# Moving a second gate rank, one attention stage and eight squares in a fused attention and two-layer MoE kernel

## The chip, the cores and the metric

The kernel runs on one core of one Trainium2 chip. The metric is the device time of one execution in microseconds (us). The kernel before takes 973.56 us, the median of three runs (973.33 to 974.96).

## The reference, cut to what matters

```python
# attention over chunks of 32 queries: 8 memory keys and a window of 16 + 32 + 8 keys
scores = scale * np.matmul(q_c, k_full.transpose(0, 1, 3, 2))
scores = scores - np.max(scores, axis=-1, keepdims=True)
a = np.exp(scores)
a = a / (np.sum(a, axis=-1, keepdims=True) + 1e-09)
out[:, :, c_start:c_end] = np.matmul(a, v_full)
# dense layer, 512 -> 2048 -> 512, on 3072 tokens
h = x @ w_in
r = np.maximum(h, 0.0)
x = (r * r) @ w_out
# top-1 mixture of 8 experts, 512 -> 1024 -> 512
e_idx = np.argmax(x @ w_gate, axis=1)
out[mask] = gate_w[mask, None] * eom[mask, e, None] * (np.maximum(x[mask] @ w1[e], 0.0) @ w2[e])
```

## The kernel before, in words

Tokens go in 12 blocks of 256 (two 128-token units each). A **duo** is the attention of one block, a **block** its dense layer. Every fp32 operand of a large product is split into a high and a low part, so a product is three matmuls. Two blocks form a group: group 1 is blocks 2 and 3, and so on. The list `seq` (L844 to L850) holds the work **items** (block, f), where f is one of 16 strips of the hidden layer. Items 0 to 31 are group 0, items 32 to 63 group 1, then 32 for each group to item 191; from item 192 on come pairs of 128-token tiles for one expert, then single tiles ("slots") to the end.

The main loop (L1114 to L1129) writes the order of every engine by hand; each engine runs its instructions in that order. For item n it issues: the first product `mm1_both` (12 matmuls, for two blocks at once, at every second item), work put `ahead`, the item's `relu`, then everything planned for n in `todo`, and last `mm2`, the second product (6 matmuls) of item n - 2. `relu` is on ScalarE (ACT) the relu `r` (L418) and the rounded square `gh` (L430), and on VectorE (DVE) the square `g` (L428) and the residual `gl` (L432). For items below 24 the square `g` is on ACT too (L426): at that time DVE also converts the weights (`split_w_or` L336 and L340, `split_w_lo` L354; `split_w_hi` L349 is on ACT).

`plan_duo(b, s, m, t, v)` places the attention of a block: scores (128 small matmuls of TensorE, PE, L158; maximum L187 and subtraction L192 on DVE, exponential L208 on ACT) at item s, the norm (L214 to L220, DVE) at m, the transposes (L231, PE) at t, the second attention product `av` (128 small matmuls, L256) at v. `plan_gate(b, y, l, c, r)` places the gate of a finished block: transposes, logits, choice, and `gate_rank` at r (L520): two small matmuls (L525, L526) give each token its place in its expert's list, seven small DVE operations follow, and two indirect DMAs from GpSimd (POOL, L537) scatter 128 rows of 8 bytes each into `listd` in HBM. `prepare` (L971) runs at item 23.

In group 1 (n = 32) the rank of the second gate stands at n + 27 and the second duo's `av` at n + 29; in groups 2 to 4 at n + 26 and n + 29.

Of the kernel before, what the change touches and what calls it, by code (L numbers as in the profile page):

```python
# [8 lines left out]
F32 = mybir.dt.float32  # L9
F32R = mybir.dt.float32r  # L10
BF16 = mybir.dt.bfloat16
# [6 lines left out]
P = 128  # L18
# [3 lines left out]
NE = 8  # L22
F2 = 1024
BLK = 256
NB = NT // BLK
TPB = BLK // P
# [16 lines left out]
C_ID, C_U, C_RANK, C_BASE, C_LT, C_ROW, C_SIG, C_TOK, C_ODD, C_NUM = 0, 128, 256, 264, 273, 435, 444, 467, 491, 506  # L43
# [11 lines left out]
def chunk_attention_relu2_moe_top1_kernel(ctx: ExitStack, tc, qk, vv, qt, kv, w_in, w_out, wg, wexp, consts, out):  # L55
    nc = tc.nc
# [9 lines left out]
    rp = ctx.enter_context(tc.tile_pool(name="rp", bufs=1))  # L66
# [6 lines left out]
    cst = cpool.tile([P, NCONST], F32, name="cst")  # L73
    ident = cst[:, C_ID : C_ID + P]
    wg_sb = cpool.tile([P, KC, 32], F32, name="wg_sb")
    before = cpool.tile([P, P], BF16, name="before")
# [289 lines left out]
    class Block:  # L366
# [52 lines left out]

        def relu_g(self, f):  # L420
            b = self.b
            early = at[b, f] < 24
            r = self.r
            g = gp.tile([P, BLK], F32, tag="g", name=f"g{b}_{f}")
            if early:
                nc.scalar.activation(g, r, ACTF.Square)  # L426
            else:
                nc.vector.tensor_tensor(g, r, r, op=ALU.mult)  # L428
            gh = gp.tile([P, BLK], F32R, tag="gh", name=f"gh{b}_{f}", bufs=3)
            nc.scalar.activation(gh, r, ACTF.Square)  # L430
            gl = gp.tile([P, BLK], F32R, tag="gl", name=f"gl{b}_{f}", bufs=3)
            nc.vector.tensor_tensor(gl, g, gh.bitcast(F32), op=ALU.subtract)  # L432
            self.g[f] = gh, gl
# [50 lines left out]
        def gate_choose(self):  # L484
            b = self.b
            ps = ps_h.tile([P, D], F32, tag="h", name=f"psg{b}")[:, : TPB * P]
            ps = ps.rearrange("p (t k c) -> p t k c", t=TPB, k=KC)
            for t in range(TPB):
                nc.tensor.transpose(
                    ps[:, t].rearrange("p k c -> p (k c)"), self.lt[:, t * P : t * P + P], ident  # L490
                )
            lg = rp.tile([P, TPB, 16], F32, tag="lg", name=f"lg{b}")
            nc.vector.tensor_reduce(
                out=lg, in_=ps.rearrange("p t k c -> p t c k")[:, :, 0:16, :], axis=AX.X, op=ALU.add
            )

            def small(name, *shape, dt=F32):
                return rp.tile([P, TPB, *shape], dt, tag=name, name=f"{name}{b}")

            mx, d, ev, first = small("gm"), small("gd", NE), small("gv", NE), small("gf")  # L500
            nc.vector.tensor_reduce(out=mx, in_=lg[:, :, 0:NE], axis=AX.X, op=ALU.max)
            nc.vector.tensor_tensor(d, lg[:, :, 0:NE], mx.unsqueeze(2).to_broadcast([P, TPB, NE]), op=ALU.subtract)
            rank = cst[:, C_RANK : C_RANK + NE].unsqueeze(1).to_broadcast([P, TPB, NE])
            nc.vector.scalar_tensor_tensor(ev, d, 0.0, rank, op0=ALU.is_ge, op1=ALU.mult)
            nc.vector.tensor_reduce(out=first, in_=ev, axis=AX.X, op=ALU.max)
            self.oh = small("oh", NE, dt=BF16)
            nc.vector.tensor_tensor(self.oh, ev, first.unsqueeze(2).to_broadcast([P, TPB, NE]), op=ALU.is_equal)

            ex, se, og, so = small("ge", NE), small("gs"), small("go", NE), small("gt")
            nc.scalar.activation(ex, d, ACTF.Exp)  # L510
            nc.vector.tensor_tensor(og, lg[:, :, NE : 2 * NE], self.oh, op=ALU.mult)
            nc.vector.tensor_reduce(out=so, in_=og, axis=AX.X, op=ALU.add)
            nc.scalar.activation(so, so, ACTF.Exp, scale=-1.0)
            nc.vector.tensor_reduce(out=se, in_=ex, axis=AX.X, op=ALU.add)
            nc.vector.tensor_scalar_add(so, so, 1.0)
            nc.vector.scalar_tensor_tensor(se, se, EPS, so, op0=ALU.add, op1=ALU.mult)
            nc.vector.reciprocal(ent[:, b * TPB : (b + 1) * TPB, 1].bitcast(F32), se)
# [333 lines left out]
    at = {bf: n for n, bf in enumerate(seq)}  # L851
# [3 lines left out]
    def plan(n, fn, *args):  # L855
        todo.setdefault(n, []).append((fn, args))

    def plan_duo(b, s, m, t, v, last=None):
        d = duos[b]
        plan(s, d.scores)  # L860
        plan(m, d.norm)
        plan(t, d.transpose_a)
        plan(v, d.av)
        if last is None:
            plan(v, d.transpose_x_copy)
        else:
            ahead[last] = d.transpose_x_copy
        if b + 1 < NB:
            plan(s + 1, duos[b + 1].load_q, 0)
            plan(s + 1, duos[b + 1].load_q, 1)  # L870
        if 2 < b < NB - 1:
            plan(v + 1, duos[b + 1].load_kv, 1)
        if b < NB - 2:
            plan(v + 2, duos[b + 2].load_kv, 0)

    def plan_gate(b, y, l, c, r):
        bl = blocks[b]
        plan(y, bl.gate_transpose)
        plan(l, bl.gate_logits)
        plan(c, bl.gate_choose)  # L880
        plan(r, bl.gate_rank)
# [17 lines left out]
    plan(bits[14] + 1, duos[3].load_kv, 0)  # L899
    plan(bits[15] + 1, duos[3].load_kv, 1)  # L900
    plan(23, lambda: prepare())
    n = at[2, 0]
    plan_duo(2, n - 8, n - 7, n - 4, n - 3)
    plan_duo(3, n + 1, n + 2, n + 5, n + 6)
    plan_gate(0, n + 7, n + 9, n + 15, n + 18)
    plan_duo(4, n + 11, n + 13, n + 15, n + 17)
    plan_gate(1, n + 19, n + 23, n + 25, n + 27)
    plan_duo(5, n + 21, n + 23, n + 25, n + 29, last=n + 30)
    for g in range(2, GROUPED - 1):
        n = at[2 * g, 0]  # L910
        plan_gate(2 * g - 2, n + 3, n + 5, n + 11, n + 15)
        plan_duo(2 * g + 2, n + 7, n + 9, n + 11, n + 13)
        plan_gate(2 * g - 1, n + 15, n + 17, n + 23, n + 26)
        plan_duo(2 * g + 3, n + 19, n + 21, n + 23, n + 29, last=n + 30)
    n = at[NB - 2, 0]
    plan_gate(NB - 4, n + 3, n + 4, n + 6, n + 9)
    plan_gate(NB - 3, n + 6, n + 8, n + 10, n + 12)
    n = at[NB, 0]
    plan_gate(NB - 2, n + 2, n + 3, n + 4, n + 6)
    plan_gate(NB - 1, n + 4, n + 5, n + 7, n + 8)  # L920
    pairs = [Pair(p) for p in range(NP)]
    slot = [Slot(s) for s in range(NS)]
    entries = pairs + slot
# [3 lines left out]
    last = at[NB, 0] - NF  # L927
# [12 lines left out]
    for p in range(NP):  # L940
        n = at[NB + p, 0]
# [24 lines left out]
    n = at[NB, 0]  # L966
# [4 lines left out]
    def prepare():  # L971

        nc.sync.dma_start(wg_sb, wg)
        nc.vector.tensor_copy(before, cst[:, C_U : C_U + P])
        nc.gpsimd.tensor_copy(base, cst[:, C_BASE : C_BASE + NE + 1])
        nc.gpsimd.tensor_copy(ent[:, :, 0], cst[:, C_TOK : C_TOK + NU])
        fill = tp.tile([P, ROWS // P, 2], I32, tag="t2", name="fill")
        nc.gpsimd.memset(fill[:, :, 0], NT)
        nc.gpsimd.memset(fill[:, :, 1], 0)
        nc.sync.dma_start(listd.rearrange("(p r) c -> p (r c)", p=P), fill.rearrange("p r c -> p (r c)"))  # L980
        zero = tp.tile([1, D], F32, tag="t2", name="zero")
        nc.gpsimd.memset(zero, 0.0)
        nc.sync.dma_start(ydram[NT : NT + 1, :], zero)

    with tc.manual_schedule():
# [4 lines left out]
        a, b = (0,), (1,)  # L990
# [276 lines left out]
```

## Time and profile before

| what | value |
| --- | --- |
| median of three runs | 973.56 us |
| profiled execution, its own time | 975.07 us |
| its span, first to last instruction | 973.3 us |
| PE busy | 951.2 us (98%) |
| DVE busy | 603.4 us (62%) |
| ACT busy | 450.2 us (46%) |
| POOL busy | 95.9 us (10%) |

The page's 40 slices show PE at 9 tenths or more nearly everywhere; the few 8s are at the start and at the fifth and tenth slices. Each engine's share is an average over stages: DVE stands at 9 tenths in the first four slices, at about 4 to 5 in the middle, and at 9 at the end. Times in the rows below count from the first instruction.

### The profile page before, as it was taken

The numbers are of one execution on the slowest core, as the hardware profiler recorded it, in microseconds if no ns is written. First come the engines' busy times: TensorE is split into PE (matmuls) and PEld (weight loads), VectorE is DVE, ScalarE is ACT, GpSimd is POOL, SyncE is SP. The second block draws the span as 40 slices with busy tenths as digits, with TensorE's granted clock in tenths as the row PEclk, the third lists the DMA queues.
The fourth block names the chain that finished last, engine by engine and source line by source line (L and its number), as shares of the span: only waits on it lengthen the run. The fifth ranks groups of instructions, "written<-read, shape, count | busy, mean of one in ns | idle before, by whom it ended". The sixth has DMA issues, their size and how long they took to land. (4 is left out here: it accounts for less than half of the span.)

```text
span 973.3 us, 19449 instructions
## 1 busy us (share of the span) xinstructions
PE 951.2 (98%) x7862; PEld 795.8 (82%) x7862; DVE 603.4 (62%) x1134; ACT 450.2 (46%) x808; POOL 95.9 (10%) x92
## 2 busy tenths in 40 slices
PE   8999899998999999999999999999999999999997
PEld 5787689877888888888888878888999999888885
DVE  6899753552455345544545344658776666799995
ACT  4687433322332333323333223544554454688885
POOL 0000000000000000000000001002222212122221
PEclk9999999998999999999999999999999999999999
DMA  9566422214120222103010104452775666553531
GB/s 357 180 232 238 151 102 110 88 23 87 66 88 23 52 80 69 63 5 127 23 45 1 45 1 173 173 217 66 297 303 227 231 221 243 187 198 130 216 123 42
DMA packets 30992, 129.06 MB, mean 133 GB/s; under 512 B 8559, under 2 KB 9071, under 8 KB 19122
## 3 DMA queue, kind: packets, MB, share of 16 engines
q1 hardware_dynamic: 25650, 113.84, 32.1%
q0 software_dynamic: 5248, 13.92, 4.2%
q8 instruction: 64, 1.05, 0.5%
q14 instruction: 30, 0.25, 0.1%
HBM read 142.19 MB, written 13.61 MB: 160 GB/s over the span
## 5 line engine op out<-in xcount | busy, mean ns | idle before, releaser
L386 PE MATMUL ph<-xhi,wi 128*128 128x512 f32 x688 | 213.6, 391 | 1.0 <-issue 0.7
L428 DVE TENSOR_TENSOR g<-r 128x256 f32<-128x256 f32 x168 | 70.8, 422 | 187.4 <-ACT r L418 187.4
L418 ACT ACTIVATE r<-ph 128x256 f32<-128x256 f32 x192 | 72.1, 375 | 238.9 <-PE ph L386 192.7
L443 PE MATMUL py<-wo,gh 128*128 128x512 f32 x384 | 157.1, 409 | 4.4 <-ACT gh L430 4.4
L386 PEld LDWEIGHTS ph<-xhi,wi 128*128 128x128 f32 x688 | 130.0, 189 | 29.7 <-DVE wi L354 1.1
L444 PE MATMUL py<-wo,gh 128*128 128x512 f32 x384 | 151.0, 393 | 0.0
L445 PE MATMUL py<-wo,gl 128*128 128x512 f32 x384 | 150.8, 393 | 0.0
L386 PE MATMUL ph<-xlo,wi 128*128 128x512 f32 x344 | 134.1, 390 | 0.0
L680 DVE TENSOR_TENSOR x<-raw,x 128x1024 fp32r<-128x1024 f32 x88 | 103.2, 1221 | 7.0 <-ACT x L679 5.4
L432 DVE TENSOR_TENSOR gl<-g,gh 128x256 fp32r<-128x256 f32 x192 | 81.6, 425 | 24.8 <-ACT gh L430 1.6
L680 DVE TENSOR_TENSOR p<-raw,p 128x1024 fp32r<-128x1024 f32 x64 | 78.2, 1221 | 22.3 <-ACT p L679 21.7
L443 PEld LDWEIGHTS py<-wo,gh 128*128 128x128 f32 x384 | 72.6, 189 | 21.1 <-ACT gh L430 5.2
L679 ACT CAST x<-raw 128x1024 fp32r<-128x1024 f32 x88 | 87.3, 1057 | 0.0
L445 PEld LDWEIGHTS py<-wo,gl 128*128 128x128 f32 x384 | 72.6, 189 | 16.2 <-DVE gl L432 0.4
L430 ACT ACTIVATE gh<-r 128x256 fp32r<-128x256 f32 x192 | 80.0, 416 | 11.2 <-PE py L444 3.0
L537 POOL DMA_INDIRECT listd<-ent,idx x24 | 25.2, 1051 | 590.5 <-DVE idx L535 341.1
L444 PEld LDWEIGHTS py<-wo,gh 128*128 128x128 f32 x384 | 72.9, 190 | 12.6
L386 PEld LDWEIGHTS ph<-xlo,wi 128*128 128x128 f32 x344 | 64.9, 189 | 13.7
L679 ACT CAST p<-raw 128x1024 fp32r<-128x1024 f32 x64 | 66.6, 1041 | 0.0
L831 PE MATMUL po<-x,ht 128*128 128x512 f32 x264 | 65.4, 397 | 0.6 <-DVE ht L821 0.6
L701 POOL DMA_INDIRECT out<-o,slots x27 | 36.0, 1335 | 209.4 <-ACT o L697 91.4
L831 PEld LDWEIGHTS po<-x,ht 128*128 128x128 f32 x264 | 48.1, 188 | 10.2 <-DVE ht L821 1.0
(229 smaller groups left out, 1453.8 us busy)
## 6 DMA issues: line engine op xcount, KB each, us to landing
raw<-in_wexp SPq DMA_DIRECT2D x82, 1024.0 KB
kv<-in_kv SPq DMA_DIRECT2D x19, 1024.0 KB
raw_o<-in_w_out SPq DMA_DIRECT2D x8, 1024.0 KB
raw_i<-in_w_in SPq DMA_DIRECT2D x7, 1024.0 KB
ydram<-y SPq DMA_DIRECT2D x24, 256.0 KB
q<-in_qt SPq DMA_DIRECT2D x20, 256.0 KB
qk<-in_qk SPq DMA_DIRECT2D x4, 768.0 KB
v<-in_vv SPq DMA_DIRECT2D x2, 1024.0 KB
```

The lines of the kernel that those rows point to most:

```text
L386: nc.tensor.matmul(ph.rearrange("p (s c) -> p s c", s=2), lhsT=w_in_part(w, f, k), rhs=x[:, s, k, :], start=(n == 0), stop=(n == 11),)
L418: nc.scalar.activation(self.r, self.ph, ACTF.Relu, scale=WSCALE)
L428: nc.vector.tensor_tensor(g, r, r, op=ALU.mult)
L430: nc.scalar.activation(gh, r, ACTF.Square)
L432: nc.vector.tensor_tensor(gl, g, gh.bitcast(F32), op=ALU.subtract)
L443: nc.tensor.matmul(self.y[t], lhsT=gh[:, s], rhs=w_out_part(wh, f), start=(f == 0), stop=False)
L444: nc.tensor.matmul(self.y[t], lhsT=gh[:, s], rhs=w_out_part(wl, f), start=False, stop=False)
L445: nc.tensor.matmul(self.y[t], lhsT=gl[:, s], rhs=w_out_part(wh, f), start=False, stop=(f == NF - 1))
L679: nc.scalar.copy(w[:, 0], t)
L680: nc.vector.tensor_tensor(w[:, 1], t, w[:, 0].bitcast(F32), op=ALU.subtract)
L701: nc.gpsimd.indirect_dma_start(out=out, out_offset=bass.IndirectOffsetOnAxis(ap=slots[:, c, 0:1].bitcast(U32), axis=0), in_=self.y[t], in_ ...
L831: nc.tensor.matmul(self.po, lhsT=self.ht[:, part, f, :], rhs=w[:, wp, j * D : j * D + D], start=(f == 0 and part == 0 and wp == 0), stop=( ...
```

## The change

The square `g` of items 24 to 31 goes from DVE to ACT. Duo 2's scores go from item 24 to 25 and its norm from 25 to 26; its transposes (28) and `av` (29) stay. In group 1 the second gate's logits go from n + 23 to n + 21 and its rank from n + 27 to n + 30; duo 5's scores go from n + 21 to n + 23, its norm from n + 23 to n + 24, its transposes from n + 25 to n + 27. In groups 2 to 4 the rank of the second gate goes from n + 26 to n + 30, one item behind `av`. After the groups, the rank of block 10 goes from item 198 to 199 and the choice of block 11 from 199 to 198, so the one-hot tile `oh` gets a second buffer. A cast in `prepare` goes from DVE to POOL.

```diff
         def relu_g(self, f):
             b = self.b
-            early = at[b, f] < 24
+            early = at[b, f] < 32
...
-            def small(name, *shape, dt=F32):
-                return rp.tile([P, TPB, *shape], dt, tag=name, name=f"{name}{b}")
+            def small(name, *shape, dt=F32, bufs=1):
+                return rp.tile([P, TPB, *shape], dt, tag=name, name=f"{name}{b}", bufs=bufs)
...
-            self.oh = small("oh", NE, dt=BF16)
+            self.oh = small("oh", NE, dt=BF16, bufs=2)
...
     n = at[2, 0]
-    plan_duo(2, n - 8, n - 7, n - 4, n - 3)
+    plan_duo(2, n - 7, n - 6, n - 4, n - 3)
     plan_duo(3, n + 1, n + 2, n + 5, n + 6)
     plan_gate(0, n + 7, n + 9, n + 15, n + 18)
     plan_duo(4, n + 11, n + 13, n + 15, n + 17)
-    plan_gate(1, n + 19, n + 23, n + 25, n + 27)
-    plan_duo(5, n + 21, n + 23, n + 25, n + 29, last=n + 30)
+    plan_gate(1, n + 19, n + 21, n + 25, n + 30)
+    plan_duo(5, n + 23, n + 24, n + 27, n + 29, last=n + 30)
     for g in range(2, GROUPED - 1):
         n = at[2 * g, 0]
         plan_gate(2 * g - 2, n + 3, n + 5, n + 11, n + 15)
         plan_duo(2 * g + 2, n + 7, n + 9, n + 11, n + 13)
-        plan_gate(2 * g - 1, n + 15, n + 17, n + 23, n + 26)
+        plan_gate(2 * g - 1, n + 15, n + 17, n + 23, n + 30)
         plan_duo(2 * g + 3, n + 19, n + 21, n + 23, n + 29, last=n + 30)
...
     n = at[NB, 0]
-    plan_gate(NB - 2, n + 2, n + 3, n + 4, n + 6)
-    plan_gate(NB - 1, n + 4, n + 5, n + 7, n + 8)
+    plan_gate(NB - 2, n + 2, n + 3, n + 4, n + 7)
+    plan_gate(NB - 1, n + 4, n + 5, n + 6, n + 8)
...
-        nc.vector.tensor_copy(before, cst[:, C_U : C_U + P])
+        nc.gpsimd.tensor_copy(before, cst[:, C_U : C_U + P])
```

## Rows read from the trace of the kernel before

**Rows 1.** The page, part 1: busy time, share and instructions of each engine.
```profile
PE 951.2 (98%) x7862; PEld 795.8 (82%) x7862; DVE 603.4 (62%) x1134; ACT 450.2 (46%) x808; POOL 95.9 (10%) x92
```

**Rows 2.** Waits of PE and POOL: line, what for, total us, times, longest us.
```profile
PE py L443 <- ACT gh L430: 4.4, 2, 3.6
PE ph1p L731 <- DVE gl1p L742: 0.8, 1, 0.8
...
POOL listd L537 <- DMA listd<-ent,idx: 40.5, 11, 7.5
```

**Rows 3.** Timeline around duo 2, 99 to 116 us: start, duration, engine, line, operation.
```profile
99.75 0.22 DVE L974 CAST before<-cst 128x128 bf16<-128x128 f32 x1
...
103.48 1.23 DVE L354 TENSOR_TENSOR wo<-ws_o,wo 128x1024 fp32r<-128x1024 f32 x1 [0.23 <-ACT wo L349]
...
104.63 1.22 DVE L187 TENSOR_REDUCE mx<-pss 128x16 f32<-128x1024 f32 x1
...
107.37 1.06 ACT L208 ACTIVATE e<-e 128x1024 f32<-128x1024 f32 x1 [3.92 <-DVE e L204]
108.33 0.36 ACT L418 ACTIVATE r<-ph 128x256 f32<-128x256 f32 x1
...
109.20 0.78 PE L443 MATMUL py<-wo,gh 128*128 128x512 f32 x1 [3.59 <-ACT gh L430]
...
109.63 1.21 DVE L214 TENSOR_REDUCE sm<-e 128x16 f32<-128x1024 f32 x1
...
111.37 1.22 DVE L220 TENSOR_TENSOR e<-e,rs 128x1024 f32<-128x1024 f32 x1
...
115.02 1.03 PE L231 MATMUL psa<-cst,e 128*128 128x128 f32 x8
```

**Rows 4.** The square on ACT, by line and shape: xcount, busy us, mean ns.
```profile
L426 ACT ACTIVATE g<-r 128x256 f32<-128x256 f32 x24 | 10.1, 419 | 0.8
```

**Rows 5.** Stretches of eighteen large matmuls: length, busy by engine (instructions), PE clock, DMA.
```profile
283.44:287.65 4.21, 4.21 (x26) 3.49 (x19) 1.22 (x1) 1.01 (x1) 0.00 (x0) 1.00 0.69 247
200.20:205.35 5.15, 4.44 (x27) 3.41 (x19) 2.37 (x2) 0.00 (x0) 0.96 (x1) 1.00 0.52 77
231.14:237.37 6.23, 6.23 (x20) 4.97 (x19) 0.00 (x0) 0.01 (x1) 0.00 (x0) 0.65 0.86 49
109.18:115.00 5.82, 5.80 (x18) 4.62 (x19) 4.73 (x9) 1.34 (x4) 0.00 (x0) 0.71 0.02 9
```

**Rows 6.** Five `av`, L256 alone: stretch, length, PE and PEld busy (instructions), clock.
```profile
281.44:283.44 2.00, 1.98 (x128) 1.96 (x128) 1.00 0.00 0
225.24:231.14 5.90, 3.27 (x128) 2.86 (x128) 0.79 0.03 3
331.98:334.67 2.69, 2.27 (x128) 2.15 (x128) 1.00 0.01 0
433.50:436.24 2.74, 2.30 (x128) 2.18 (x128) 1.00 0.07 6
535.13:537.41 2.28, 2.26 (x128) 2.15 (x128) 1.00 0.03 4
```

**Rows 7.** Timeline of group 1: scatters, the stopped `av`, item 63's relu.
```profile
203.16 0.96 POOL L537 DMA_INDIRECT listd<-ent,idx  x1 [7.52 <-DMA listd<-ent,idx]
...
222.15 0.97 POOL L537 DMA_INDIRECT listd<-ent,idx  x1 [18.02 <-DVE idx L535]
...
228.85 0.44 PE L256 MATMUL psx<-e,kv 64*64 64x32 f32 x5 [1.99 <-issue]
...
239.01 0.37 ACT L418 ACTIVATE r<-ph 128x256 f32<-128x256 f32 x1
```

**Rows 8.** DMA queue of instructions in 185:186, 200:201 and 228:229 us: packets, MB, share.
```profile
q8 instruction: 1, 0.02, 6.7%
q8 instruction: 1, 0.02, 25.2%
q8 instruction: 1, 0.02, 13.5%
```

## The prediction

> **What bounds the kernel now.** I read the busy times first: PE is busy 951.2 of 973.3 us [rows 1]. So work that merely moves between DVE, ACT and POOL gains nothing; a gain must come out of the 22 us in which PE stands still, or out of time at the lower of its two clocks. The waits [rows 2] say where PE stands still in the middle: 3.6 us of a second product for `gh`, and 0.8 us for a residual in the first pair; to these come waits of `av` for "issue", where no engine is named: PE had no instruction to run [rows 7]. The timeline puts the first at 105.6 to 109.2 us, item 25 [rows 3]. To price the others I cut stretches of equal work. A second product, a first product (eighteen large matmuls) take 4.21 us at clock 1.00; the rows count a few small matmuls that overlap the edges [rows 5]. An `av` that nothing disturbs takes 2.00 us; the four that follow the second gate's rank take 5.90, 2.69, 2.74 and 2.28 [rows 6]. The chain that ended last reaches back only 0.5% of the span and is of no help.
>
> **Why those four `av` are long.** In group 1 the scatter of the rank is issued at 222.15, `av` starts at 225.26, and PE then waits 1.99 us for issue with the product unfinished [rows 7]. PE's instructions come by DMA in packets of 0.02 MB. In a quiet microsecond one took 6.7% of 16 engines, 1.07 us; at 228 us 13.5%, 2.16 us; at 200 us, behind the first gate's scatter, 25.2%, 4.03 us [rows 8]. `av` needs 256 instructions (128 matmuls, 128 weight loads) in 2 us, so it is the one place where a slow packet shows. I take it that the scatter slows the packet.
>
> The Trainium skill (Runtime: NRT & Kernel Launch, section Instruction fetch mechanics) says that instructions come in blocks of 256 by a DMA queue of the engine's own, and that crossing a block is mostly hidden. The rows of the quiet `av` agree; the 1.99 us do not. If fetches were always hidden, the rank's place would not matter; that is the fourth case below.
>
> **The change, part by part.**
>
> *Rank behind `av`, groups 1 to 4.* The rank now stands one item later than `av`: `av`, a second product, a first product (2.0 + 4.2 us), then its two matmuls; some 3 us on come the scatters, about 11 us after `av` began. The four `av` go to 2.00: 3.90 + 0.69 + 0.74 + 0.28 = 5.61 us. Behind the long one the next eighteen matmuls run at clock 0.65, partly at 1.2 GHz, and take 6.23 instead of 4.21 [rows 5]: 2.02 more. What the moved rank costs: PE's two matmuls, DVE's seven operations and POOL's two DMAs are the same, later. On DVE they now stand behind the low part of the next block's input and ahead of the residual of item n + 31, which PE needs over 3 us after. They take one of two PSUM banks of the first product, so the product of item n + 32 must wait until both relus of n + 30 have read theirs: today the second of them ends at 239.01 + 0.37 [rows 7], 2.0 us after that product's end at 237.37 [rows 5]; PE comes back after its two second products, 2.7. Nothing behind POOL waits; SP is not passed by them. I take zero, between 0 and 0.5 us a group, since the margin is 0.7.
>
> *Duo 5's scores at n + 23, logits at n + 21.* In the stretch behind today's scores PE loses 5.15 - 4.21 = 0.94 us [rows 5], where the packet took 4.03 us [rows 8] between two scatters of the first rank. The scores (256 instructions too) come two items, some 6 us, later, near 205 us; in their place come the logits with 32 instructions. The loss goes: 0.94 us, if the second scatter, at 203.16 behind a wait of 7.52 for the first [rows 7], comes earlier too. That is the weak step; its other end is the third case. SP's two loads of the next queries move with the scores; the next duo needs them over 50 us later.
>
> *Duo 2's scores one item later, squares on ACT.* Here I expect the stall to move, not to go. Walk along DVE and ACT before: low part of the last weight at 103.48, maximum 104.63, exponential 107.37, relu 108.33, PE released 109.20; the norm runs from 109.63 to 111.37 + 1.22 = 112.59; the transposes start at 115.02 [rows 3]. After, the relu of item 25 is ahead of the exponential, so item 25 no longer waits. But the transposes stay at item 28, and PE runs in order. DVE does the low part 0.14 earlier, since the cast (0.22 us, [rows 3]) is gone, then the residual of item 25 (about 0.34: some 0.42 less the 0.08 by which DVE's operations overlap, as 103.48 + 1.23 against 104.63), then maximum and subtraction: the exponential starts at 107.37 + 0.19 = 107.56. Now item 26's relu, square and `gh` follow it on ACT: the relu 0.96 later, at 108.52, as before, and the three end near 109.7 (419 ns for the square, [rows 4], and less by the overlap); the residual follows on DVE, and the norm starts near 110.0 instead of 109.63 and ends near 113.0. PE meanwhile has only the second product of item 25 and the first of item 28 more to do: from 105.4, 4.2 us, to 109.6. It then waits for the norm, 3.4 us in place of 3.59. The transposes start at 113.0, 2.0 us earlier than before. But before, the clock fell during the stall, and the eighteen matmuls behind it took 5.82 instead of 4.21 at clock 0.71 [rows 5]: 1.6 us. After a stall of 3.4 I expect the same, behind the transposes. Gain 2.0 - 1.6 = 0.4; between 0 (the clock stays low as long as in the 6.23 row) and 2.0 (it does not fall). I take 0.4, since 3.4 is nearest to 3.59.
>
> The eight squares leave DVE and come to ACT, 8 x 0.42 = 3.4 us: beside PE's work, except the one in the walk. The cast on POOL runs near the start, where POOL waits for constants; its first reader is the rank at item 50: zero.
>
> *Last gates.* The same operations in another order over items 198 to 200. PE waits 0.8 us today at item 201 for a residual of item 200 that DVE does late [rows 2]. The choice of block 11 (13 small DVE operations, some 2.6 us) now delays the residual of item 199 instead, so the wait comes one item sooner. On POOL the two gathers of pair 2 pass ahead of the rank's scatters: earlier, which hurts nobody. Zero, between -0.8 and +0.8.
>
> **Sum.** 0.4 + 0.94 + 5.61 + 2.02 + 0 = 9.0 us. PE is busy without gaps behind these places, so what is won is kept to the end. Against the profiled execution: span 973.3 to 964.3, its own time 975.07 to about 966.1. The median of the runs lies 1.5 lower; 973.56 - 9.0 = 964.6.
>
> **The rivals.**
>
> *Second case, the stall of duo 2 shrinks or goes.* For it: 2.0 us if the clock holds; against it: the norm's chain above. 1.6 to 5 us more, 959.6 to 963.
>
> *Third case, a scatter hits something else.* The first two scatters of the program were slow (the first pair's wait is 7.52 us [rows 7]; the other ten that are put down so have 3.3 on average, (40.5 - 7.5) / 10, [rows 2]). If the second still goes out at 203.16, the scores at 205 start 2 us behind it, as `av` started 3 us behind 222.15. Price as there: 3.90 + 2.02 = 5.9; 970.5. Against it: today's scores lie between the first two scatters, and only the stretch behind them lost time.
>
> *Fourth case, the rank is not the cause.* Then `av` stays long where it stands and only 0.4 + 0.94 are won: 972.2, within 0.2%. Against it: the undisturbed `av` of the even duos, which have no scatter ahead of them.
>
> *Fifth case, slower.* The scatters now fall 11 us behind `av`, where PE starts the next group. A packet fetched there could be slow and leave PE dry in the dense stretch, in each of four groups. Price: 3.90 a group, 15.6 - 9.0 = 6.6 slower, 980.2; it decides from 9.0 / 4 = 2.25 us a group. Against it: eighteen matmuls and as many loads take 4.21 us there, some 9 instructions in a microsecond, so 4 us are 36 of the 256 of an `av`, and the first gates' scatters in groups 2 to 4 lie in such stretches today without a wait of PE.
>
> **How the numbers follow.** Chances: the sum 0.61, second case 0.13, third 0.14, fourth 0.06, fifth 0.06. The range reaches from inside the second case to beyond the third, 961.5 to 971, and leaves out some of the second, the fourth and the fifth. About 0.2% (1.95 us) is what a measurement of this kernel can tell from no change: faster is below 971.6, so the first three cases (with a little of the third lost): 0.86; same, the fourth and that little: 0.08; slower 0.06.
>
> **What would show it.** Right: all four second `av` at 2.00 us; no issue wait in group 1; the large matmuls behind it at clock 1.00; a wait of PE of about 3.4 us at the transposes of duo 2 (L231, for the norm L220) instead of at L443; the 0.8 us of the first pair one item sooner. Wrong: a stopped `av` with no scatter in flight (the cause was another), a wait for issue at duo 5's scores or at the head of a group (it moved), or no wait at duo 2's transposes (my chain is too long).

## The result and the profile after

| | before | after |
| --- | --- | --- |
| median of five runs each, same chip | 974.96 us (973.33 to 976.94) | 966.83 us (965.34 to 968.53) |
| profiled execution, its own time | 975.07 us | 966.68 us |
| its span | 973.3 us | 964.7 us |

The ratio is 0.992, 95% interval 0.990 to 0.994: faster by 8.1 us. Forecast were 964.6 us, 9.0 below the median known then, and a range of 961.5 to 971.0.

The page after, part 1, answers [rows 1]: for the same instructions PE is busy 4.5 us less (more of them at the full clock), and of the span of 964.7 it stands still 18.0 us instead of 22.1.

```profile
PE 946.7 (98%) x7862; PEld 792.5 (82%) x7862; DVE 600.0 (62%) x1125; ACT 452.9 (47%) x816; POOL 97.8 (10%) x93
```

The second `av` of groups 1 to 4 in the kernel after, L256 alone (columns as in [rows 6]), then the eighteen large matmuls behind the first of them and behind duo 5's scores (as [rows 5]):

```profile
223.53:225.55 2.02, 2.00 (x128) 1.96 (x128) 1.00 0.00 0
324.36:326.38 2.02, 2.00 (x128) 1.96 (x128) 1.00 0.00 0
425.17:427.19 2.02, 2.00 (x128) 1.96 (x128) 1.00 0.04 8
526.08:528.10 2.02, 2.00 (x128) 1.96 (x128) 1.00 0.01 4
...
225.55:229.77 4.22, 4.22 (x24) 3.30 (x19) 0.00 (x0) 0.03 (x1) 0.00 (x0) 1.00 0.71 254
...
205.81:210.03 4.22, 4.22 (x25) 3.49 (x20) 2.56 (x3) 1.06 (x1) 0.00 (x0) 1.00 0.33 34
```

All four take 2.00 us where [rows 6] has 5.90, 2.69, 2.74 and 2.28, and the stretches are at 4.22 where [rows 5] has 6.23 and 5.15. The waits of PE after, against [rows 2]:

```profile
PE psa L231 <- DVE e L220: 3.2, 1, 3.2
...
PE ph1p L731 <- DVE gl0p L742: 0.8, 1, 0.8
...
PE ph2p L731 <- DVE gl2p L742: 0.3, 1, 0.3
```

The stall of duo 2 has moved to the transposes, the first pair's wait now stands one item sooner, and the last line is new. To see where the time went I put the same PE instruction of both traces side by side. The lead of the kernel after grows and shrinks so:

| place | lead | what lies between |
| --- | --- | --- |
| item 24 | 0.33 us | the start, which differs from execution to execution |
| item 30 | 0.73 us | duo 2: 0.40 |
| behind duo 5's scores | 1.72 us | 1.03, less 0.04 for small waits ahead of them |
| item 64 | 7.47 us | group 1's `av` and the clock: 5.75 |
| first pair | 9.18 us | three `av`: 1.71 |
| pair 2 and the end | 8.64 us | given back: 0.55 |

### The profile page after: what moved, and what is told of

Its sections match the earlier page's. It is cut to its first block, busy times and chain, and to the rows that moved or that the text cites. A ratio compares the mean times of both kernels' runs of the same rounds, so it can differ in the third digit from the quotient of the medians.

```text
span 964.7 us, 19444 instructions
## 1 busy us (share of the span) xinstructions
PE 946.7 (98%) x7862; PEld 792.5 (82%) x7862; DVE 600.0 (62%) x1125; ACT 452.9 (47%) x816; POOL 97.8 (10%) x93
## 5 line engine op out<-in xcount | busy, mean ns | idle before, releaser
L428 DVE TENSOR_TENSOR g<-r 128x256 f32<-128x256 f32 x160 | 67.4, 421 | 183.7 <-ACT r L418 183.7
```

## The experiments

My theory at first was that of the prediction: a scatter in flight slows the packets of PE's instructions and so stops `av`; duo 2's stall is a matter of order; the last gates are free. That it goes by the second scatter of a rank, and not by the packets, came out of the runs. The rivals stand in the expectations. Where medians are given, "before" is the kernel before, run on the same chip beside them.

**The rank alone.** The kernel before with the rank of the second gate at n + 30, nothing else.

```diff
-    plan_gate(1, n + 19, n + 23, n + 25, n + 27)
+    plan_gate(1, n + 19, n + 23, n + 25, n + 30)
...
-        plan_gate(2 * g - 1, n + 15, n + 17, n + 23, n + 26)
+        plan_gate(2 * g - 1, n + 15, n + 17, n + 23, n + 30)
```

> The kernel before with one edit: the second gate's rank (matmuls, DVE operations and scatters) at n + 30 in groups 1 to 4; duo 5's scores stay at n + 21. Theory (the scatter in flight slows the packets of PE's instructions): all four av take 2.00 us instead of 5.90, 2.69, 2.74 and 2.28, the large matmuls behind the first run at clock 1.00; the stretch behind duo 5's scores, which stands between the two scatters of the first gate, keeps its 5.15 us; about 7.6 us less than before, 0.992. Rival (the av are long for a reason of their own, such as where a block of 256 instructions ends): they stay long, within 0.2% of before.

Measured: 967.65 us against 975.37, ratio 0.994 (0.992 to 0.996). All four `av` are at 2.00, the stretch behind the first at 4.21, the one behind duo 5's scores is still long, and the wait for `gh` of 3.6 us and the first pair's wait stay where they were. Of the windows:

```profile
198.36:203.37 5.01, 4.48 (x23) 3.41 (x19) 2.38 (x2) 0.00 (x0) 0.97 (x1) 1.00 0.52 80
...
225.11:229.32 4.21, 4.21 (x24) 3.30 (x18) 0.00 (x0) 0.02 (x1) 0.00 (x0) 1.00 0.73 251
```

The rank is worth nearly all of the change; the 0.8 to 0.9 us of the first row are gone only where the scores and logits of duo 5 have moved too (4.22 us in the kernel after). No run moves one of these two alone.

**The scatters alone, first attempt.** The kernel before; only the writing of the scatters is moved to n + 30 in the program.

```diff
             nc.vector.tensor_copy(idx, pos)
+            self.idx = idx
+            if b not in (1, 3, 5, 7):
+                self.gate_scatter()
+
+        def gate_scatter(self):
+            b, idx = self.b, self.idx
             for t in range(TPB):
```

> The kernel before with one edit: the rank's matmuls and DVE operations stay at n + 27 and n + 26, only the two indirect DMAs of POOL are issued from item n + 30. Theory (scatter): as with the whole rank moved, four av at 2.00 us, about 7.6 us less than before. Rival (PE's two small matmuls with other weights, or the DVE operations ahead of av, are the cause): av stays at 5.90, 2.69, 2.74 and 2.28, no gain.

Measured: 975.09 us, ratio 1.000 (0.999 to 1.002); the four `av` 4.29, 2.69, 2.52 and 2.50. That tells nothing of the scatter, because it did not move: POOL is idle there and waits for `idx` alone, so the scatters ran at 220.86 and 227.74 as before. Written later in the order of an idle engine is not later in time.

**The scatters alone, by their data.** As above, but the cast to `idx` on DVE goes to n + 30 too; the rank's two matmuls and its other DVE operations stay.

```diff
-            nc.vector.tensor_copy(idx, pos)
+            self.idx, self.pos = idx, pos
...
+        def gate_scatter(self):
+            b, idx = self.b, self.idx
+            nc.vector.tensor_copy(idx, self.pos)
```

> The kernel before, where of the second gate of groups 1 to 4 only the last DVE operation (the cast to idx) and the two scatters behind it go to item n + 30; the rank's two matmuls and its other six DVE operations stay at n + 27 and n + 26. The scatters cannot start before idx is there, so they now truly go out behind av. Theory (the scatter slows the packet of instructions that av needs): all four second av take 2.00 us, the eighteen matmuls behind the first of them 4.21 instead of 6.23, and the time is 5.6 + 2.0 = 7.6 us below the kernel before, as with the whole rank moved (7.7 there); the stretch behind duo 5's scores keeps its 5.0 to 5.15 us. Rival (it is the rank's matmuls or its work on DVE that make av long): av stay at some 2.3 to 5.9 us and the time is within 1 us of the kernel before.

Measured: 967.92 us against 971.72, ratio 0.997 (0.995 to 0.998); the kernel before was quicker on this chip (968.79 to 976.47 in 26 runs), so the 3.8 us are less than expected. The trace is as the theory has it: four `av` at 2.00, 4.21 behind the first, 5.75 behind duo 5's scores (where nothing had moved).

```profile
226.55:228.59 2.04, 2.02 (x128) 1.96 (x128) 1.00 0.00 0
327.37:329.41 2.04, 2.02 (x128) 1.96 (x128) 1.00 0.00 0
428.24:430.28 2.04, 2.02 (x128) 1.96 (x128) 1.00 0.03 8
529.13:531.17 2.04, 2.02 (x128) 1.96 (x128) 1.00 0.01 4
...
228.59:232.80 4.21, 4.21 (x23) 3.48 (x20) 0.00 (x0) 0.04 (x1) 0.00 (x0) 1.00 0.68 243
```

So it is the scatters (with the cast that releases them), not the rank's matmuls or its other work on DVE, that make `av` long, in groups 2 to 4 at least. There all 15 second `av` of the five traces with the scatters at their old place take 2.28 us or more, and all 27 of the nine traces with the scatters behind `av` take 2.00. For group 1 one trace shows less, as the next run tells.

**Why the first scatters are slow.** The kernel before with two dummy scatters of pad rows at item 23.

```diff
+        for t in range(2):
+            nc.gpsimd.indirect_dma_start(
+                out=listd,
+                out_offset=bass.IndirectOffsetOnAxis(ap=warm[:, t : t + 1].bitcast(U32), axis=0),
+                in_=fill[:, t, :],
+                in_offset=None,
+            )
```

> The kernel before with two more scatters of 128 empty entries each into rows of the list that nobody uses, issued at item 23, long ahead of the first rank. Theory (the first two pairs of scatters are slow, 7.5 and 5.9 us, because they are the first of the program): now the extra ones are slow, the first gate's second scatter comes 4 to 5 us behind its first instead of 8.6, the stretch of 5.15 us behind duo 5's scores shrinks to about 4.2 and av of group 1 from 5.90 to about 2.7 like the later ones. Rival (they are slow for where or when they write): 8.6 us, 5.15 us and 5.90 us stay.

Measured: 969.41 us in one run. POOL's rows (the last bracket is the wait between the two scatters of a pair):

```profile
112.19 1.02 POOL L988 DMA_INDIRECT listd<-fill,warm  x1 [4.61 <-DMA listd<-fill,warm]
...
201.91 0.96 POOL L537 DMA_INDIRECT listd<-ent,idx  x1 [7.40 <-DMA listd<-ent,idx]
...
231.11 0.96 POOL L537 DMA_INDIRECT listd<-ent,idx  x1 [7.54 <-DMA listd<-ent,idx]
```

The first two gates are not slow for being first; why they wait 7 us where later ones wait 3 stays open. And here group 1's `av` took 2.00 us untouched, while in the kernel before it took 5.90 and in the scatter run 4.29: much the same order of work is hit or spared from one execution to the next. The two shifted kernels further down are spared too. So in five traces in which this `av` begins 3.1 us behind the rank's first scatter, it loses 3.9 us, 2.3 us and three times nothing.

**Duo 2, norm and transposes later too.** On the kernel after.

```diff
-    plan_duo(2, n - 7, n - 6, n - 4, n - 3)
+    plan_duo(2, n - 7, n - 5, n - 2, n - 1)
```

> The changed kernel with duo 2's norm one item later (27), its transposes at item 30 instead of 28 and its av at 31 instead of 29. Theory (the stall moved to the transposes, which stand in PE's order ahead of work that is ready): the wait of 3.2 us at the transposes and the half clock behind it go; a new wait of about 0.65 us at the first product of item 32, whose input the av now delivers late; the first product of item 32 starts near 121 instead of 125.56, so about 4 us less than the changed kernel, 0.996. Rival (DVE is the bound of this stage, so any order loses the same): the wait turns up elsewhere with about 3 us, and the time stays within 1 us.

Measured: 963.82 us against 975.37, ratio 0.990 (0.988 to 0.993); that is 3.0 below the kernel after, which ran beside another set of the kernel before (974.96), where some 4 were expected. In the traces this stage is 3.9 us shorter: the second product of item 30 begins at 124.09 for 126.99, in an execution that was 0.99 us behind ahead of duo 2. The waits of PE have no line for `psa` L231 <- `e` L220 any more:

```profile
PE ph2p L731 <- DVE gl2p L742: 0.6, 1, 0.6
PE ph L407 <- DVE xlo L300: 0.6, 1, 0.6
```

The stall was one of order: with more matmuls ahead of the transposes it costs 0.6 us instead of 3.2 and the clock behind it.

**Squares back on DVE.** On the kernel after.

```diff
-            early = at[b, f] < 32
+            early = at[b, f] < 24
```

> The changed kernel with the squares of items 24 to 31 back on DVE. By the walk of the prediction the square of item 26 stood in the chain ahead of the norm on ACT (419 ns); on DVE it runs beside the rounded square. So the wait at duo 2's transposes is some 0.3 us shorter, 2.9 instead of 3.2 us, and nothing else moves. Rival (DVE is short of time in this stretch, which is why the squares had to leave it): DVE's 8 squares of 0.42 us delay the exponential's input and the norm, and the wait is 3.6 us or longer, or residuals of later items (L432) make PE wait.

Measured: 967.32 us in one run, and the wait is 3.6 us: my expectation fell, the rival holds. DVE's timeline, first of the kernel after, then of this one (start, duration, line):

```profile
104.18 0.42 DVE L432 TENSOR_TENSOR gl<-g,gh 128x256 fp32r<-128x256 f32 x1
104.52 1.22 DVE L187 TENSOR_REDUCE mx<-pss 128x16 f32<-128x1024 f32 x1
...
111.47 1.22 DVE L220 TENSOR_TENSOR e<-e,rs 128x1024 f32<-128x1024 f32 x1
```

```profile
104.06 0.42 DVE L428 TENSOR_TENSOR g<-r 128x256 f32<-128x256 f32 x1
104.61 0.43 DVE L432 TENSOR_TENSOR gl<-g,gh 128x256 fp32r<-128x256 f32 x1
104.95 1.22 DVE L187 TENSOR_REDUCE mx<-pss 128x16 f32<-128x1024 f32 x1
...
111.71 1.23 DVE L220 TENSOR_TENSOR e<-e,rs 128x1024 f32<-128x1024 f32 x1
```

This execution ran 0.14 us ahead here (its scores began at 98.22 against 98.36), so the square ahead of the maximum puts that back by 0.43 + 0.14 = 0.57 us and the last operation of the norm by 0.24 + 0.14 = 0.38, which is the longer wait. I had looked at the square of item 26 alone, on ACT; that of item 25, on DVE, weighs more. The squares on ACT carry all of duo 2's 0.40 us: with them on DVE the lead over the kernel before is 0.44 us ahead of duo 2 and 0.30 behind it. That is one execution of each; the run with the last gates as before, which has this stage as in the kernel after, differs from it by 0.08 us. The one time of 967.32 us tells nothing here. (The page has DVE at 6, 8, 9 and 9 tenths in the first four slices, not at 9 in all four, and at 7 in the fifth, where duo 2 lies.)

**Last gates as before.** On the kernel after.

```diff
-    plan_gate(NB - 2, n + 2, n + 3, n + 4, n + 7)
-    plan_gate(NB - 1, n + 4, n + 5, n + 6, n + 8)
+    plan_gate(NB - 2, n + 2, n + 3, n + 4, n + 6)
+    plan_gate(NB - 1, n + 4, n + 5, n + 7, n + 8)
```

> The changed kernel with the last two gates as before (rank of block 10 at item 198, choice of block 11 at 199). Theory (the new order of the last gates puts the second pair's store and its gathers later on POOL, and so causes the new wait of 0.3 us for gl2p and the 0.55 us that the changed kernel gives back at pair 2): the wait for gl2p is gone, the wait of pair 1 (0.8 us) stands one item later again, and the time is some 0.5 us below the changed kernel's 8.1 to 8.5 us gain, 9 us below the kernel before. Rival (the 0.55 us come from the moved ranks, or from the chance of one execution): a wait for gl2p stays and the gain does too.

Measured: 965.68 us against 971.72, ratio 0.994 (0.993 to 0.996). These times can't test half a us against the kernel after, which was timed beside another 974.96; the traces can. The wait for `gl2p` is gone, the first pair's stands at its old item. POOL and DVE at pair 2, first after, then with the gates as before:

```profile
674.11 1.05 POOL L537 DMA_INDIRECT listd<-ent,idx  x1 [5.45 <-DMA listd<-ent,idx]
...
681.27 0.99 POOL L701 DMA_INDIRECT out<-o,slots  x1 [4.81 <-DVE p L680]
...
689.25 1.41 DVE L695 TENSOR_SCALAR o<-po,slots 128x512 f32<-128x512 f32 x2 [0.38 <-DMA out<-o,slots]
```

```profile
671.49 0.98 POOL L537 DMA_INDIRECT listd<-ent,idx  x1 [6.15 <-DMA listd<-ent,idx]
...
678.35 0.99 POOL L701 DMA_INDIRECT out<-o,slots  x1 [4.33 <-DVE p L680]
...
688.51 1.39 DVE L695 TENSOR_SCALAR o<-po,slots 128x512 f32<-128x512 f32 x2
```

With the gathers ahead, the last scatter of the two gates comes 2.6 us later on POOL, and the second store of the pair behind it 2.9 us later (681.27 for 678.35; the execution with the gates as before ran 0.4 us behind, so 3.0 and 3.3 at equal work); DVE's scaling of the next pair waits 0.38 us for that store to land, and PE for DVE. From the fourth first product of pair 2 to the fifth it is 3.28 us after and 2.82 here. The four other traces with the new order lose at the same place (3.56, 3.58, 3.79 and 4.27); in all nine with the old one it is 2.82.

**Both together.** Duo 2 later, last gates as before.

> The changed kernel with duo 2's norm, transposes and av at items 27, 30 and 31, and the last two gates as before. If both gains add: no wait of PE at duo 2's transposes, 0.6 us at the first product behind, no wait for gl2p; 3.0 (duo 2 moved later: 963.82 against 966.83) and 0.5 (last gates) below the changed kernel, 963.3, 11.7 to 12 us below the kernel before. If the last gates are worth nothing: as with duo 2 alone, 963.8.

Measured: 962.19 us (961.27 to 963.62) against 971.72, ratio 0.991 (0.989 to 0.993), the quickest of all; the waits at duo 2's transposes and for `gl2p` are both gone. Beside the last-gates run on the same chip it is 3.5 us quicker, as duo 2 alone was 3.0 below the kernel after. That is 1.1 below the 963.3 expected, but only 9.5 below the kernel before, not 11.7 to 12, since that one is quicker on this chip.

**A scatter ahead of another `av`.** On the kernel after, the first gate's rank in groups 2 to 4 goes three items ahead of the first duo's `av`.

```diff
-        plan_gate(2 * g - 2, n + 3, n + 5, n + 11, n + 15)
+        plan_gate(2 * g - 2, n + 3, n + 5, n + 7, n + 10)
```

> The changed kernel, where the first gate's choice and rank in groups 2 to 4 go from items n + 11 and n + 15 to n + 7 and n + 10, three items ahead of the first duo's av at n + 13, the distance that the second gate's rank had from its av before. These three av took 2.00 us in every kernel so far. Theory (a scatter shortly ahead of an av makes it long, wherever it stands): they take 2.3 to 2.8 us now, as their neighbours did before (0.69 + 0.74 + 0.28 = 1.7 us in all), so the time is some 1.7 us above the changed kernel, 6.5 to 7 below the kernel before. Rival (only the place at a group's end is touchy, where packets, the duo's loads or the clock differ): the three av stay at 2.00 and the time stays.

Measured: 966.49 us; the theory as I had put it fell. The three `av`, L256 alone, and the instruction queue at the second of them (373.5 to 374.5 us):

```profile
271.79:273.83 2.04, 2.02 (x128) 1.96 (x128) 1.00 0.01 0
372.63:374.75 2.12, 2.07 (x128) 1.96 (x128) 1.00 0.10 8
473.60:475.64 2.04, 2.02 (x128) 1.96 (x128) 1.00 0.11 9
```

```profile
q8 instruction: 1, 0.02, 19.2%
```

A packet took 3.07 us (19.2% of 16 engines in 1 us) beside an `av` that lost at most 0.08 us. So a slow packet does not starve PE by itself. Either the place of the packets matters, or something else does.

**The packets shifted.** On the kernel before, the first warm-up matmuls are cut into smaller ones, so that all packets of instructions move by 72 or by 168 instructions against the work (the second diff: 96 matmuls of 64 columns).

```diff
-        keep_busy(12)
+        for i in range(48):
+            nc.tensor.matmul(spin[:, i % 4, :], lhsT=ones, rhs=ones, start=True, stop=True)
```

> The kernel before, where the first twelve warm-up matmuls of 512 columns (L1008) are 48 of 128 columns: the same columns, but 36 more matmuls and 36 more weight loads, so every packet of 256 PE instructions is asked for 72 instructions earlier in the program. Counted in the trace of the kernel before, the packets that go with the second av of groups 2, 3 and 4 are asked for 10 instructions ahead of av, 86 and 182 instructions into it. Theory (PE runs dry because a packet asked for near av is slowed by a scatter): the packet of group 2 now falls 82 instructions ahead of av, some 8 us and before the scatter, so this av goes from 2.69 to 2.00 us, while group 3's (14 into av) stays near 2.7. Rival (the scatter stops PE by itself, wherever the packets fall): all three stay near 2.7, 2.6 and 2.3 us, the stop begins 90 to 93 instructions into av, as before, and ends 1.3 us behind the issue of the second scatter. The time is that of the kernel before within its spread in both cases.

> As the kernel with 72 instructions more, with 96 warm-up matmuls of 64 columns, so 168 instructions more. The packets of groups 2, 3 and 4 are now asked for 78 instructions into av, 82 ahead of it, and 14 into it. Theory of the slowed packet: group 2's av stays near 2.7 us, group 3's goes to 2.00. Rival (the scatter by itself): all three stay near 2.7, 2.6 and 2.3 us, the stop 90 to 93 instructions into av.

Measured: 976.46 and 975.26 us against 975.24; the cut warm-up itself costs time before 35 us, and in return group 1's `av` happened to be spared in both (with 72, duo 5's scores were hit instead, 5.92 us). The second `av` of groups 2, 3 and 4: 2.90, 2.68 and 2.28 us with 72, 2.55, 2.61 and 2.55 with 168. None went to 2.00, so the packets are not the cause. In the kernel with 168 no packet of instructions moved from 426 to 436 us (the only queue there is the scatter's), and the `av` at 433.67 was stopped all the same:

```profile
q0 software_dynamic: 64, 0.00, 0.5%
```

```profile
332.16 1.07 POOL L537 DMA_INDIRECT listd<-ent,idx  x1 [2.95 <-DMA listd<-ent,idx]
332.26 0.78 PEld L256 LDWEIGHTS psx<-e,kv 64*64 64x64 f32 x47 [0.35 <-issue]
...
333.45 0.77 PE L256 MATMUL psx<-e,kv 64*64 64x32 f32 x37 [0.30 <-issue]
...
433.60 1.05 POOL L537 DMA_INDIRECT listd<-ent,idx  x1 [2.98 <-DMA listd<-ent,idx]
433.67 0.78 PEld L256 LDWEIGHTS psx<-e,kv 64*64 64x64 f32 x46 [0.35 <-issue]
...
434.88 0.54 PEld L256 LDWEIGHTS psx<-e,kv 64*64 64x64 f32 x28 [0.43 <-issue]
...
534.96 0.96 POOL L537 DMA_INDIRECT listd<-ent,idx  x1 [2.88 <-DMA listd<-ent,idx]
535.12 0.78 PEld L256 LDWEIGHTS psx<-e,kv 64*64 64x64 f32 x45 [0.35 <-issue]
...
536.24 0.88 PEld L256 LDWEIGHTS psx<-e,kv 64*64 64x64 f32 x51 [0.34 <-issue]
```

Read the three pairs of times: PE goes on 1.28 to 1.31 us behind the start of the **second** scatter's issue on POOL (333.45, 434.88, 536.24; in the kernel with 72 it is 335.00 for an issue at 333.69), whenever `av` began; and before it stops it gets some 45 matmuls with their weight loads, in 0.67 us. My reading is that while POOL issues the second scatter no new instruction reaches PE, and that it lives on about 90 that it has. The times show when PE goes on; that reading of the stop is argued, not shown. Where the issue begins 0.26 and 0.51 us behind the start of `av` (with 72, and in the next run), PE should by it get some 62 and 78 matmuls (45, and 64 more per us), and got 49 and 53. And the second scatter goes out as soon as the first has landed, so no run tells its issue from that landing. In numbers, a dense stretch of small matmuls loses 0.62 us + (issue of the second scatter - start of `av`), if that is positive. That gives, for the 21 `av` of seven kernels with a scatter near (the second one of groups 2 to 4 of the kernel before, of the scatter run, the dummy run and the two shifted ones, the first one in the run above and the next), the measured length within 0.12 us in 20; the exception is 271.81 of the run above (0.75 us expected, none lost), which I can't explain. The rule was fitted to these same `av` afterwards: no run was forecast by it, and in four of the 20 it expects no loss.

**The same shift on the kernel with the other `av`.** 72 instructions more on the kernel with the first gates' ranks ahead.

> The kernel with the first gates' ranks three items ahead of the first duo's av (whose three av ran undisturbed, 2.00, 2.08 and 2.00 us, with the scatters as near as in the kernel before), with the 72 more PE instructions of warm-up. The packets were asked for 198, 40 and 138 instructions into these av, now 126 into, 32 ahead and 66 into them. If it was the place of the packets that spared them, at least the second or third of them is long now (2.3 us or more), and the time some 1 us longer. If not, they stay at 2.00 to 2.1 us, and what spared them is something else.

Measured: 971.22 us, 4.7 above the kernel without the shift (on another chip). 3.1 us of this are lost by the scores of duo 2 already, at the start. The three `av`:

```profile
276.45:279.61 3.16, 2.56 (x128) 2.28 (x128) 1.00 0.01 0
378.42:380.46 2.04, 2.02 (x128) 1.96 (x128) 1.00 0.01 1
479.32:481.48 2.16, 2.14 (x128) 2.08 (x128) 1.00 0.11 8
```

The one that is long is not the one I had named by its packet. The rule of the second scatter's issue has it: issued 0.51 us behind the start of the first `av` (276.98 against 276.47), so 2.00 + 0.62 + 0.51 = 3.13, measured 3.12; 1.18 and 0.61 us ahead of the others, so 2.00 and 2.01, measured 2.00 and 2.12.

## Why the prediction was right, and where it was not

**Four `av` and the clock: right in size, wrong in cause.** 5.61 and 2.02 us were put down, 5.75 + 1.71 = 7.46 came. The step that failed is "I take it that the scatter slows the packet". The slow packets are real, but they go beside the stop and don't make it: an `av` ran on beside a packet of 3.07 us, another stopped with no packet in flight. What the runs show for groups 2 to 4 in its place is that the scatters stop `av`, and that PE goes on 1.28 to 1.31 us behind the start of the second one's issue; one `av` in 21 breaks the rule. The wrong step did no harm because the edit was the same by either cause: take the scatter away from `av`. The Trainium skill (Runtime: NRT & Kernel Launch, section Instruction fetch mechanics), whose rule of hidden fetches I had weighed and set aside, also gives PE an instruction memory of 128 KiB, 2048 instructions; by an estimate from that, a packet some us late is not missed, and the `av` beside the packet of 3.07 us agrees. For group 1 the cause is not settled: there the stop (226.86 to 228.85, [rows 7]) ended before the second scatter was issued at 228.99, and the slow packet of [rows 8] began only at 228.06, inside the stop, and took 2.16 us, beyond its end.

The size was in part luck. Of the 7.63 us, 5.92 (3.90 and 2.02) are group 1's, priced from one execution, and this stop comes and goes: with the same distances it took 3.9 us, 2.3 us and three times nothing, in five traces; in the nine traces with the scatters behind it, it took nothing. The prediction has no chance for an `av` that is spared. Where it is spared, as in the one execution with the dummy scatters (969.41 us), the change is worth some 2.7 us (against 966.68, one execution each). How often it is hit no run counts.

**Duo 5's scores: right in size, the reason open.** I made the 0.94 us depend on an earlier second scatter and called it the weak step. The scatter did not come earlier (202.31, in an execution 0.7 us ahead, for 203.16), yet 1.03 us were won. POOL and PE after, then PE before:

```profile
202.31 0.97 POOL L537 DMA_INDIRECT listd<-ent,idx  x1 [7.35 <-DMA listd<-ent,idx]
204.37 1.35 PEld L158 LDWEIGHTS pss<-kv,q 64*32 64x32 f32 x128 [0.35 <-issue]
```

```profile
202.59 0.65 PE L386 MATMUL ph<-xhi,wi 128*128 128x512 f32 x2 [0.71 <-issue]
```

The scores stand 2.06 us behind the second issue, and its 1.3 us are over; in all seven traces with the scores there (1.73 to 2.70 us behind it) none is stopped. But what cost 0.94 us before was a wait that ended at 202.59, ahead of that issue at 203.16, so the rule of the second scatter does not explain it. Nor does it exclude the third case, which set scores 2 us behind a second scatter beside an `av` 3 us behind a first one: at the old place, between the two, the kernel with 72 more instructions had its scores stopped for 4.01 us, again with an end ahead of the second issue:

```profile
205.86 0.76 PE L158 MATMUL pss<-kv,q 64*32 64x64 f32 x33 [4.01 <-issue]
...
206.44 0.96 POOL L537 DMA_INDIRECT listd<-ent,idx  x1 [8.94 <-DMA listd<-ent,idx]
```

What stops PE between the two slow scatters of the first two gates stays open.

**Duo 2: right.** The stall moved to the transposes, 3.2 us for 3.4, they start at 112.83 for 113.0, and of the 2.19 us by which they start sooner (0.33 of it is the start of the program) the clock behind them leaves 0.40, for 0.4. Of the walk, the exponential stood at 107.26 (107.56 forecast) and the norm at 109.72 (110.0), which with the 0.33 of the start is 107.59 and 110.05:

```profile
107.26 1.06 ACT L208 ACTIVATE e<-e 128x1024 f32<-128x1024 f32 x1 [3.21 <-PE py L445]
...
109.72 1.21 DVE L214 TENSOR_REDUCE sm<-e 128x16 f32<-128x1024 f32 x1
...
112.83 1.94 PE L231 MATMUL psa<-cst,e 128*128 128x128 f32 x8 [3.19 <-DVE e L220]
```

What I had not seen is the part of the squares in it, which the run with them back on DVE gave.

**Last gates: inside the bounds, but not zero.** The first pair's wait moved as told. The step that failed is "On POOL the two gathers of pair 2 pass ahead of the rank's scatters: earlier, which hurts nobody". I asked who waits for the gathers, not what is queued behind the scatters: the stores are. Price 0.55 us, between the -0.8 and 0.8 put down.

**The sum.** 0.33 (start) + 0.40 + 1.03 + 5.75 + 1.71 - 0.55 = 8.67 us against 8.64 in the traces; the forecast of 9.0 lacked the last term. That 966.83 us lies 2.2 above 964.6 has a second part: the kernel before itself stood at 974.96 beside the kernel after, 1.4 above the three runs that I had. The fifth case, packets at the head of a group, did not come: the first products of the groups keep their 4.2 us.

## What to carry to other kernels

Keep long runs of small matmuls clear of indirect DMAs on GpSimd, by data dependencies and not by the order in which they are written; here a stretch was clear from 1.3 us behind the issue of a rank's second scatter, and between two scatters that are far apart it was hit in some executions and spared in others. A stop that comes and goes should be priced from more than one execution. When a DMA on an in-order queue is overtaken, price what is queued behind it, not only who reads it. And when an edit gives the expected time, undo its parts all the same: here the sum was right with the cause wrong, and a rank put just ahead of another `av`, which by the forecast cause should have cost 1.7 us, cost nothing in one trace and 1.1 us in the next.

## What the runs showed of the hardware that I had not expected

- When GpSimd issues the second of two scatters of 128 x 8 bytes (0.96 to 1.18 us in its row) near a dense stretch of small matmuls in groups 2 to 4, PE stops after some 90 instructions (0.67 us at 128 instructions a us; 98 and 106 where the issue came later) and goes on 1.28 to 1.31 us behind the start of that issue; one stretch of 21 was spared against this. The Trainium skill (Perfetto Trace Analysis, section DMA Instruction — SWDGE (GPSIMD)) says that such a row ends when the last descriptor is generated; PE came back 0.1 to 0.3 us behind that end. Which path is blocked no run here shows.
- Between a gate's two scatters POOL waited 6.7 to 8.9 us for the first gate, 5.3 to 7.6 for the second and 2.5 to 4.1 for those of groups 2 to 4; when other scatters went before them, the first two still took 7.40 and 7.54. No run shows why.
- The start varies: the first duos' last scores (L158) began between 26.36 and 28.14 us in the eleven kernels with the same start, at 29.07 and 30.21 with 72 more instructions, at 34.05 with 168 more. Comparing the same instruction of two traces, stage by stage, takes this out; comparing times does not.
